# Strassen's algorithm for the output matmul of a fused attention and SwiGLU kernel on one Trainium2 core

## The chip, the core and the metric

The kernel runs on one core of a Trainium2 chip. The metric is device time in microseconds (us), as the median of several runs. "Span" is the time from the first to the last instruction in the trace of one profiled run; it is some 1.8 us shorter than the time that the same run reports. PE is TensorE's matmul stream, PEld its weight loads, DVE is VectorE, ACT is ScalarE, POOL is GpSimd, SP is SyncE. PSUM is the memory to which TensorE writes its results (the tiles `ps_D` of the traces), in banks; SBUF is the memory from which it reads. An eviction is VectorE's copy of a result out of PSUM.

## The reference

Sigmoid attention over 8 batches of 12 heads (448 tokens, 64 columns each), then a SwiGLU feed-forward layer on the 3584 tokens of 768 columns:

```python
scores = scale * np.matmul(q, k.transpose(0, 1, 3, 2)) - np.log(S)
attn_out = np.matmul(1.0 / (1.0 + np.exp(-scores)), v)
x = attn_out.transpose(0, 2, 1, 3).reshape(B * S, H * D)      # 3584 x 768
g = x @ w_gate                                                # 768 -> 1536
out = (g * sigmoid(g) * (x @ w_val)) @ w_out                  # 1536 -> 768
```

## The kernel before

The program is one long stream of matmuls on TensorE with everything else fitted beside it. For each pair of batches `pb` it computes two blocks of the first feed-forward matmul (12 units `ffn1(b, f)` per batch) and then the output matmul (7 units `ffn2(pb, m)`, one per tile of 128 tokens). The attention is cut into 24 "jobs" of 4 heads with 7 chunks each, and from the second batch on a "visit", usually three or four chunks of attention (two visits make a job), is set between two units whenever a program clock says so. I call the stretches F0 to F7 (first matmul of batch 0 to 7) and O0 to O3 (output matmul of pair 0 to 3).

```python
def ffn2(pb, m):                       # one output tile: 2 halves x 12 = 24 matmuls of 384 columns
    D = Banked("o")                    # a PSUM tile of two banks, out of a ring of four
    for half in range(2):
        for f in range(NF):            # NF = 12
            D.write(nc.tensor.matmul(out=D.t[:, half, :hw],
                                     lhsT=h[:, m * 128:(m + 1) * 128],          # hT of (pb, f)
                                     rhs=wo16[f // FW][:, f % FW, half * hw:(half + 1) * hw], ...), half, ...)
    for half in range(2):              # VectorE scales the bank into SBUF
        D.read(nc.vector.tensor_scalar(out=osb[:, hs], in0=D.t[:, half, :hw], scalar1=HREC, ...), half)
    for i in range(2):                 # stores: GpSimd's queue, SP's at the end
        (nc.sync if last else nc.gpsimd).dma_start(out=dsts[i], in_=osb[i * 64:(i + 1) * 64, :])

def fetch(n):                          # q, k, v of job n from HBM; all from GpSimd's queue
    load(n, 0, G); load(n, 1, G); load_v(n)

def ready(n):                          # casts of q and k on GpSimd, then DMA transposes on SP
    cast(n, 0, G); cast(n, 1, G)
    if n >= NPE:
        trans_dma(n, 0); trans_dma(n, 1)

FU1, FU2 = 2.26, 3.9                   # us booked for a unit
FIRST, PER = f1_end[0] - 5.0, 38.5     # first visit, and the time booked per batch of visits
...
begin[(6, 0)] += [lambda: ready(7)]    # what is issued at which chunk of which job
begin[(6, 4)] += [lambda: fetch(8)]
...
for dur, fn, args in units:            # the weave
    if vi < len(visits) and tcur >= vtime[vi]:
        attn_step(group, pvs)          # visit: attention matmuls, casts of the results to xT on VectorE
        ...
    fn(*args)
    tcur += dur
```

In the traces below each of VectorE, GpSimd and the queues of DMA issues works in program order, so what stands ahead and waits holds up all that stands behind.

## Time and profile before

| | before |
|---|---|
| time, median of 3 | 429.04 us (428.95 to 429.08) |
| span of the profiled run | 426.6 us |
| PE busy | 415.9 us, 97%, 3261 matmuls |
| VectorE busy | 204.9 us, 48% |
| GpSimd busy | 117.5 us, 28% |

The table is part 1 of the profile page. With TensorE busy 97% of the span, this kernel can gain mainly by having fewer matmuls, or by filling the start and the end. The prediction below shows the busy slices, the chain of waits and the timelines that say so.

One measure is used throughout. In an undisturbed stretch of this trace a matmul of 384 columns starts 162.5 ns after the one before it, one of 448 columns 189.2 ns, one of the attention's quarter-array matmuls 47 ns on average. I call **loss** all time between the starts of consecutive matmuls beyond that spacing, summed over a stretch; it is worked out from the matmuls' start times in the trace. Before, the losses are 14.9 us in the start (up to F0), 8.5 us in all the rest.

### The profile page before, as it was taken

The numbers are of one execution on the slowest core, as the hardware profiler recorded it, in microseconds if no ns is written. First come the engines' busy times: TensorE is split into PE (matmuls) and PEld (weight loads), VectorE is DVE, ScalarE is ACT, GpSimd is POOL, SyncE is SP. The second block draws the span as 40 slices with busy tenths as digits, with TensorE's granted clock in tenths as the row PEclk, the third lists the DMA queues.
The fourth block names the chain that finished last, engine by engine and source line by source line (L and its number), as shares of the span: only waits on it lengthen the run. The fifth ranks groups of instructions, "written<-read, shape, count | busy, mean of one in ns | idle before, by whom it ended". The sixth has DMA issues, their size and how long they took to land.

```text
span 426.6 us, 7903 instructions
## 1 busy us (share of the span) xinstructions
PE 415.9 (97%) x3261; PEld 217.6 (51%) x3261; DVE 204.9 (48%) x337; ACT 211.9 (50%) x291; POOL 117.5 (28%) x167
## 2 busy tenths in 40 slices
PE   6899999999999999999999999999999999999995
PEld 2544544545555444545555544544555545555663
DVE  2726656555324555555323556555433356555322
ACT  4966885654624755656433755746433642222000
POOL 5564346401637346000345545000221100000000
PEclk8799999999999999999999999999999999999999
DMA  8999999995699997500298996600162300000234
GB/s 301 231 277 211 210 190 208 177 247 99 152 218 174 194 174 178 115 0 2 71 229 169 226 193 164 120 0 2 23 131 71 81 0 2 0 2 0 55 94 111
DMA packets 57796, 54.38 MB, mean 127 GB/s; under 512 B 35680, under 2 KB 52448, under 8 KB 57760
## 3 DMA queue, kind: packets, MB, share of 16 engines
q0 software_dynamic: 20896, 39.20, 40.9%
q1 hardware_dynamic: 36512, 14.13, 20.3%
q8 instruction: 25, 0.41, 0.4%
q10 hardware_dynamic: 352, 0.56, 0.4%
q14 instruction: 11, 0.09, 0.1%
HBM read 47.19 MB, written 11.01 MB: 136 GB/s over the span
## 4 chain that ended last, share of the span: by engine, by line
PE 91%; ACT 3%; DVE 2%; issue 1%; DMA 1%; ACTq 0%; DVEq 0%
PE ps_D L256 50%; PE ps_D L296 26%; PE ps_D L197 8%; PE ps_D L228 7%; ACT pt L215 2%; DMA st<-in_q_dram 1%; PE ps_D L171 1%; DVE t L273 1%; ACT s L271 1%; ACT pt L212 1%; DVE T L180 0%; DVE hT L277 0%; DVE xT L237 0%; DVE xT L245 0%; ACT xT L243 0%
## 5 line engine op out<-in xcount | busy, mean ns | idle before, releaser
L215 ACT ACTIVATE pt<-ps_D,sb_t 128x896 f16<-128x896 f32 x148 | 140.3, 1014 | 84.4 <-PE ps_D L197 84.2
L256 PE MATMUL ps_D<-xT,wg 128*128 128x448 f16 x576 | 126.9, 353 | 0.9 <-ACT pt L215 0.5
L256 PE MATMUL ps_D<-xT,wv 128*128 128x448 f16 x576 | 126.4, 352 | 0.0
L296 PE MATMUL ps_D<-wo,hT 128*128 128x384 f16 x672 | 111.8, 326 | 0.0
L273 DVE TENSOR_TENSOR t<-ps_D,s 128x448 f16<-128x448 f32 x96 | 59.9, 624 | 92.3 <-ACT s L271 92.0
L271 ACT ACTIVATE s<-ps_D 128x448 f16<-128x448 f32 x96 | 52.7, 549 | 90.6 <-PE ps_D L256 80.1
L296 PEld LDWEIGHTS <-hT 128*128 128x128 f16 x672 | 64.8, 98 | 46.4 <-issue 4.3
L256 PEld LDWEIGHTS <-wg 128*128 128x128 f16 x576 | 53.7, 98 | 58.5 <-issue 12.4
L256 PEld LDWEIGHTS <-wv 128*128 128x128 f16 x576 | 56.4, 98 | 52.8 <-issue 0.3
L327 DVE TENSOR_SCALAR osb<-ps_D 128x384 f32<-128x384 f32 x55 | 30.7, 558 | 74.2 <-PE ps_D L296 71.0
L277 DVE SCALAR_TENSOR_TENSOR hT<-ps_D,t 128x448 f16<-128x448 f32 x96 | 60.0, 625 | 10.4 <-DVE t L273 0.5
L337 POOL DMA_DIRECT2D out_dram<-osb x42 | 22.4, 537 | 146.1 <-DVE osb L327 146.1
L149 POOL CAST c<-st 128x896 bf16<-128x896 f32 (+1 forms) x42 | 38.8, 936 | 63.1 <-issue 29.6
L197 PE MATMUL ps_D<-T,T 64*64 64x448 bf16 x672 | 47.4, 367 | 2.3 <-ACT T L180 1.1
L228 PE MATMUL ps_D<-pt,v 64*64 64x448 f16 x672 | 36.2, 351 | 0.3 <-ACT pt L215 0.3
L197 PEld LDWEIGHTS <-T 64*64 64x64 bf16 x672 | 16.3, 107 | 25.9 <-issue 18.2
L237 DVE CAST xT<-ps_D 128x448 f16<-128x448 f32 x24 | 15.0, 625 | 29.8 <-PE ps_D L228 23.0
L245 DVE CAST xT<-ps_D 64x448 f16<-64x448 f32 x46 | 28.6, 622 | 0.7
L228 PEld LDWEIGHTS <-v 64*64 64x64 f16 x672 | 19.9, 108 | 13.0 <-issue 1.5
L212 ACT ACTIVATE pt<-ps_D,sb_t 128x448 f16<-128x448 f32 x40 | 23.0, 631 | 0.0
L140 POOL DMA_DIRECT2D v<-in_v_dram x24 | 17.7, 738 | 0.1
L135 POOL DMA_DIRECT2D st<-in_k_dram x20 | 14.7, 736 | 3.1 <-DMA wv<-in_moe_w_val_dram 3.1
(25 smaller groups left out, 59.6 us busy)
## 6 DMA issues: line engine op xcount, KB each, us to landing
st<-in_q_dram POOLq DMA_DIRECT2D x20, 448.0 KB, 4.8
st<-in_k_dram POOLq DMA_DIRECT2D x20, 448.0 KB, 7.0
out_dram<-osb POOLq DMA_DIRECT2D x42, 192.0 KB, 3.1
v<-in_v_dram POOLq DMA_DIRECT2D x24, 224.0 KB, 8.3
wg<-in_moe_w_gate_dram POOLq DMA_DIRECT2D x4, 576.0 KB, 14.4
wv<-in_moe_w_val_dram POOLq DMA_DIRECT2D x4, 576.0 KB, 14.6
wo<-in_moe_w_out_dram POOLq DMA_DIRECT2D x4, 576.0 KB, 14.7
out_dram<-osb SPq DMA_DIRECT2D x12, 192.0 KB, 2.7
```

Source lines behind the costliest of these rows:

```text
L149: (eng.copy if eng is nc.scalar else eng.tensor_copy)(out=t.rearrange("p c h d -> p h c d"), in_=st.rearrange("p h (c d) -> p h c d", c=C) ...
L197: nc.tensor.matmul(out=sc[w * 64:(w + 1) * 64, h2, :S], lhsT=kt[r, w * 64:(w + 1) * 64], rhs=qt[r, :, w * 64:(w + 1) * 64], start=True, st ...
L212: nc.scalar.activation(out=pt[:, h2, :], in_=sc[:, h2, :S], func=SIGM, bias=sb_t, scale=qkscale), h2
L215: nc.scalar.activation(out=pt, in_=sc[:, :, :S], func=SIGM, bias=sb_t, scale=qkscale)
L228: nc.tensor.matmul(out=P[g:g + 64, h2, :S], lhsT=vt[r, h2, c * D:(c + 1) * D], rhs=pt[r, h2, :], start=(c == 0), stop=(c == C - 1),)
L245: nc.vector.tensor_copy(out=o, in_=i)
L256: nc.tensor.matmul(out=D.t[:, i, :S], lhsT=w16[f // FW][:, pr, cs], rhs=xT[(b, pr)], start=(pr == 0), stop=(pr == NP - 1),),
L271: D.read(nc.scalar.activation(out=s16, in_=D.t[:, 0, :S], func=SIGM), 0)
L273: D.read(nc.vector.tensor_tensor(out=t1, in0=D.t[:, 0, :S], in1=s16, op=MULT), 0)
L277: nc.vector.scalar_tensor_tensor(out=hT[(b // 2, f)][:, b % 2, :], in0=D.t[:, 1, :S], scalar=HSC, in1=t1, op0=MULT, op1=MULT),
L296: nc.tensor.matmul(out=D.t[:, half, :hw], lhsT=h[:, m * 128:(m + 1) * 128], rhs=wo16[f // FW][:, f % FW, half * hw:(half + 1) * hw], start ...
L327: nc.vector.tensor_scalar(out=osb[:, hs], in0=D.t[:, half, :hw], scalar1=HREC, scalar2=None, op0=MULT),
```

## The change

Its intent: a pair of token tiles, g and g+3, is computed in one group. With A the activations of the two tiles, split in two halves of the 1536 inner columns, and B the output weights, split two by two, the Winograd form of Strassen's algorithm needs 7 products where the plain one needs 8. A product is 6 matmuls, so a pair takes 42 instead of 48. There are 11 such groups: 2 in O0 (its first pair of tiles stays plain, to let the weights arrive) and 3 each in O1 to O3; the seventh tile stays plain.

The sums of activations are computed while `ffn1` of the odd batch runs: 72 sums on VectorE in units f = 6 to 11, 24 on GpSimd in units 0 to 5. The 8 sums of weights are computed once on VectorE, in O0. All output stores move to SP's queue; loads, output weights and casts get a new order; the transposes of a job stand further behind its casts; some SBUF pools shrink to make room.

```diff
+    def w_sums(s):                                 # 4 sums of 128 x 1152, called for s = 0 and 1
 ...
+        for kind in (3, 2, 1, 4):                  # b22-b12, wT3+b11, b12-b11, b21-wT2
 ...
+            nc.vector.tensor_tensor(out=t, in0=a, in1=b, op=op)
+    def h_sums(pb, f):
 ...
+        if f < HF:
+            work = ((3, a11, a21, SUB),)
+        else:
+            work = ((1, a21, a22, ADD), (2, None, a11, SUB), (4, a12, None, SUB))
+        for kind, a, b, op in work:
 ...
+            (nc.gpsimd if kind == 3 else nc.vector).tensor_tensor(out=t, in0=a, in1=b, op=op)
 ...
+    def ffn2_group(pb, g):
 ...                                                # mm(k, bank, ..): product k; the comments are added
+        mm(1, 0, True, False)                      # product 1 into bank 0: 6 matmuls
+        snap(0, o1, 0)                             # VectorE: scale bank 0 into o1, left half
+        mm(2, 1, True, True)
+        put(1, o1, 0)                              # VectorE: add bank 1 to o1, left half
+        mm(6, 0, False, False)                     # on top of product 1
+        snap(0, o1, 1)
+        mm(5, 1, True, False)
+        snap(1, o2, 1)
+        mm(7, 0, False, False)
+        put(0, o2, 1)
+        mm(3, 1, False, True)
+        put(1, o1, 1)
+        mm(4, 0, False, True)
 ...                                                # stores from SP
+                o_units += [(FU2, ffn2, (pb, g)), (0.0, w_sums, (0,)), (FU2, ffn2, (pb, g + 3)), (0.0, w_sums, (1,))]
 ...
-    FIRST, PER = f1_end[0] - 5.0, 38.5
+    FIRST, PER = f1_end[0] - 5.0, 37.3
 ...
-    begin[(6, 0)] += [lambda: ready(7)]
-    begin[(6, 4)] += [lambda: fetch(8)]
-    begin[(7, 0)] += [lambda: ready(8), lambda: fetch(9)]
+        (5, 4): ((fetch, 7), (w_out, 0)),
+        (6, 0): ((ready, 7), (w_out, 1)),
+        (6, 4): ((fetch, 8), (w_out, 2)),
+        (7, 0): ((ready, 8), (w_out, 3)),
```

## The prediction

> **What bounds the kernel now.** I read the page first: busy share per slice, then the chain of work that ended last, then the groups. After that came the tensor engine's waits and the timeline of three stretches.
>
> ```profile
> PE   6899999999999999999999999999999999999995
> DVE  2726656555324555555323556555433356555322
> PE 91%; ACT 3%; DVE 2%; issue 1%; DMA 1%; ACTq 0%; DVEq 0%
> PE ps_D L256 50%; PE ps_D L296 26%; PE ps_D L197 8%; PE ps_D L228 7%; ACT pt L215 2%; DMA st<-in_q_dram 1%; PE ps_D L171 1%; DVE t L273 1%; ACT s L271 1%; ACT pt L212 1%; DVE T L180 0%; DVE hT L277 0%; DVE xT L237 0%; DVE xT L245 0%; ACT xT L243 0%
> L296 PE MATMUL ps_D<-wo,hT 128*128 128x384 f16 x672 | 111.8, 326 | 0.0
> L327 DVE TENSOR_SCALAR osb<-ps_D 128x384 f32<-128x384 f32 x55 | 30.7, 558 | 74.2 <-PE ps_D L296 71.0
> ```
>
> Except in the first three slices and the last, PE is full. It is 91% of the chain, and the output matmul (L296) is 26%. The tensor engine's own waits sum to about 6 us, nearly all in the first 25 us. So PE instruction count sets the time, and VectorE at 48% has room on average. One matmul's "326 ns" isn't its cost, because matmuls overlap. The cost is the spacing, which the timeline of the last output phase gives through its evictions, one per 12 matmuls:
>
> ```profile
> 395.71 26.49 PE L296 MATMUL ps_D<-wo,hT 128*128 128x384 f16 x162
> 396.88 0.56 DVE L327 TENSOR_SCALAR osb<-ps_D 128x384 f32<-128x384 f32 x1 [1.16 <-PE ps_D L296]
> 398.83 0.56 DVE L327 TENSOR_SCALAR osb<-ps_D 128x384 f32<-128x384 f32 x1 [1.39 <-PE ps_D L296]
> ...
> 422.23 0.48 ACT L316 ACTIVATE oe<-ps_D 64x384 f32<-64x384 f32 x1 [27.89 <-PE ps_D L296]
> 422.75 0.56 DVE L320 TENSOR_SCALAR oe<-ps_D 64x384 f32<-64x384 f32 x1 [1.91 <-ACT oe L316]
> 423.33 0.47 SPq L324 DMA_DIRECT2D out_dram<-oe  x1
> ```
>
> 398.83 - 396.88 = 1.95 us for 12, so **162.5 ns a matmul**. After PE ends at 422.20 a tail of 4.4 us remains to 426.6. An attention visit inside an output phase looks so:
>
> ```profile
> 127.52 0.57 PE L197 MATMUL ps_D<-T,T 64*64 64x448 bf16 x8
> 127.92 1.49 PE L228 MATMUL ps_D<-pt,v 64*64 64x448 f16 x28
> 129.24 0.55 PE L197 MATMUL ps_D<-T,T 64*64 64x448 bf16 x8
> 129.53 0.62 DVE L237 CAST xT<-ps_D 128x448 f16<-128x448 f32 x1 [1.35 <-ACT pt L212]
> 129.72 4.07 PE L296 MATMUL ps_D<-wo,hT 128*128 128x384 f16 x24
> 130.17 1.26 DVE L245 CAST xT<-ps_D 64x448 f16<-64x448 f32 x2
> ```
>
> PE spends 2.2 us (127.52 to 129.72), while VectorE's three casts run from +2.0 to +3.9 us. This order matters below.
>
> **What the Trainium skill says.** (1) "TensorE: Matmul & The Clock Gate", section "Wait — 56ns, not 53.3ns?": spacing is N / 2.4 GHz plus 2.5 ns. For 384 columns that is 162.5 ns; the trace agrees. (2) "VectorE: DVE Perf Modes", section "The perf-mode tier table (the rule you actually need)": tensor_tensor on 16-bit SBUF data runs 2x, with a PSUM operand 1x. In the trace a 448-column op from PSUM takes 625 ns and a 384-column one 558, so 1.04 ns a column plus about 160 ns. A 16-bit copy of 896 takes 623 ns, i.e. half the slope. No SBUF-only tensor_tensor is in this trace. (3) "SBUF — State Buffer", section "Who interferes with whom": a VectorE instruction with two SBUF inputs and a GpSimd instruction that reads SBUF block each other. No VectorE op before has two SBUF inputs, so the trace can't show it; all the new sums do. (4) "TensorE: Matmul & The Clock Gate", section "What's actually happening": after an idle window of about 3.4 us the PE clock halves. The trace agrees loosely: the granted clock is 0.74 in 10 to 20 us, behind the gaps of the start.
>
> **The change part by part.**
> Removed: a pair of token tiles took 48 matmuls, and takes 7 products x 6 = 42. Groups: three in each of pairs 1 to 3, two in pair 0, so 11. 11 x 6 = 66 matmuls x 162.5 ns = **10.7 us off PE**, all of it on the path. This is the ceiling.
>
> Evictions: 7 instead of 4 per group, 33 more x 558 ns = 18 us of VectorE. A product is 6 x 162.5 = 975 ns, and two PSUM banks alternate. Counting from the start of a product's last matmul: eviction starts at +0.36 (first evictions above), ends at +0.92, PE sees it about 0.05 later (as at its first starts behind VectorE: 5.72 to 5.77). The bank is wanted at 7 x 162.5 = +1.14. Slack 0.17 us: undisturbed groups don't stall. Anything that keeps VectorE busy when a group begins does stall it.
>
> Sums of activations: 72 on VectorE (128x384, 16-bit), each 192 / 0.96 + 156 = 356 ns, 26 us in all. They fall in 6 units of each odd block: 1.25 + 3 x 0.36 = 2.32 us of VectorE against 12 x 189 ns = 2.27 us of PE. Just saturated; attention visits there give PE extra time about equal to their casts. With four PSUM tiles I allow 0.6 us, contention with GpSimd casts (0.94 us each) included. GpSimd's 24 sums are off the path.
>
> Sums of weights: 8 of 1152 columns, 576 / 0.96 + 156 = 756 ns. The first four lie behind a plain tile and hide. **The second four don't.** Working through the schedule (unit times against visit times: after the tile pair 0,3 the clock stands at 65.9, the visit was due at 62.9), the visit of job 9 with job 8's casts comes just ahead of them, and the first group just behind. From the visit's start: casts end +3.9, sums +6.9, the first snapshot of bank 0 +7.5. PE has done two products by +2.2 + 1.95 = +4.2 and wants bank 0. **PE waits 3.4 us.** That idles nearly a clock window, so I add 0.3 us as expected value.
>
> The same queueing with casts alone, twice (the first group of pair 1 and the third of pair 2): +4.5 against +4.2, together 0.8 us. Three groups start one three-chunk visit after the former one; their PSUM tile comes back 0.2 us late: 0.6 at most, I take 0.4.
>
> Schedule: larger units bunch visits. At the turns from pair 1 to 2 and 2 to 3, only one unit lies between visits. In 45 to 60 us, where that is so now, PE lost about 0.2 us per visit; I take 0.6. Transposes now stand behind output stores in SP's queue. Job 17's pair is issued about 2 us after its visit, lands some 6 us later (median 6.1), and is wanted 7.7 us after it: 0.6 us. Loads and output weights move, but I see slack of several us, so 0.
>
> Tail: two output tiles are stored at the end instead of one half tile. SP issues five stores at about 0.5 us each from the end of the last product, the last one near +2.0 instead of +1.1, with about 790 KB in flight: +1.1 us.
>
> Sum: -10.7 + 3.4 + 0.3 + 0.8 + 0.4 + 0.6 + 0.6 + 0.6 + 1.1 = -2.9 us, or 426.1. The losses are estimates that can overlap (PE waiting for one thing lets the others catch up), while the 10.7 us is sure. So I discount them by about a fifth and put the point at **424.6 us**.
>
> **The rivals.**
> A: the sums hide. The author tuned the visit spacing (38.5 to 37.3) for this, VectorE is half idle, and undisturbed groups have slack. Then only the tail and some tenths are lost: 418.5 to 420. Against it speaks the queue order ahead of the first group.
> B: VectorE becomes the bound in odd blocks, through sums slower than 356 ns (1x, or blocked by GpSimd), and groups stall at every bank change. At 1x a sum would take 556 ns, a unit 2.9 us, and 18 such units would give back 18 x 0.65 = 11 us: 429 to 432. The 623 ns copy speaks for 2x.
> C: SP's single queue delays stores or transposes; a missed transpose is several us of idle PE at one or two visits: 427 to 429. Now transposes land in 6 us with 12 between visits, so only the bunched turn is at risk.
>
> **Range and chances.** My sum is a mixture between A and C: 424.6, with 420.3 to 428.0 eight times in ten. Faster by over 2% needs 420.46, so losses under 2.2 us in all; with the weight sums' stall alone at 3.4 that needs my queue reading to fail: 0.14. Slower by over 2% needs B in full: 0.02. Within 2%: 0.84.
>
> **What would show it.** L296's successors should count 606 matmuls with the same spacing. PE busy falls by nearly 11 us, its idle rises by the losses. One idle of about 3.4 us, near 115 to 120 us, released by VectorE right behind the weight sums, confirms the main step; if it is absent I was wrong there, towards A. Sums of 356 and 756 ns confirm 2x; longer ones point to B. Waits inside groups without a visit ahead would refute the slack of 0.17. A PE wait for a transposed tile shows C. The tail behind the last matmul should be about 5.5 us.

## The result, and the profile after

The time is **429.68 us** (median of 4 runs, 429.44 to 429.92), beside 429.06 us for the kernel before in the same rounds (4 runs, 428.95 to 429.84). Ratios are from the fast runs of both kernels in the same rounds, and not quite the ratios of the medians: here 1.0011, with a 95% interval of 0.9993 to 1.0028. Executions over 1.5% slower than the fastest of the same kernel are left out of the means. The change gained nothing. "Within 2%" was right; the point of 424.6 us and the range to 428.0 us were wrong.

Part 1 of the page, first of the kernel before, then of the kernel after (busy us, share of the span, instructions):

```profile
PE 415.9 (97%) x3261; PEld 217.6 (51%) x3261; DVE 204.9 (48%) x337; ACT 211.9 (50%) x291; POOL 117.5 (28%) x167
```

```profile
PE 408.9 (95%) x3195; PEld 212.0 (50%) x3195; DVE 256.3 (60%) x450; ACT 212.0 (50%) x291; POOL 117.7 (27%) x149
```

The 66 matmuls are gone, and PE's busy time fell by 7.0 us, less than the 10.7 us of 66 x 162.5 ns. The span of the profiled run still grew, from 426.6 to 428.1 us. So PE now waits. Parts 2 and 4 of the page of the kernel after say where (busy tenths in 40 slices of 10.7 us each, and the chain that ended last):

```profile
PE   6899999998979999999999999999999999999994
DVE  2726656578664555558765456558865456558753
PE 76%; DVE 12%; ACT 6%; issue 3%; DMA 1%; DVEq 0%; ACTq 0%
```

PE has new dents in the tenth slice (96 to 107 us, the end of F1) and the twelfth (118 to 128 us, in O0), and apart from the last slice (the tail) nowhere else that this view resolves. The chain that set the end went through VectorE for 2% of the span before, and does for 12% now. PE's waits by releaser in the kernel after (sum in us, times, longest); the lines of the start are left out:

```profile
PE ps_D L376 <- DVE osb L387: 3.0, 3, 2.6
PE ps_D L207 <- DMA T<-c: 1.6, 1, 1.6
...
PE ps_D L449 <- DVE xT L255: 0.5, 1, 0.5
...
PE ps_D L207 <- DVE osb L462: 0.4, 1, 0.4
```

L376 is a matmul of a group, L207 one of the attention's q k matmuls, L449 one of a plain output tile. The first two lines are the largest new waits, one behind VectorE and one behind a transposed tile.

The losses by stretch, before and after:

| stretch | before, us | after, us | difference |
|---|---|---|---|
| start and F0 | 14.90 | 15.25 | +0.35 |
| F1 | 0.92 | 3.25 | +2.33 |
| O0 | 0.92 | 5.94 | +5.02 |
| F2, F3 | 2.31 | 3.63 | +1.32 |
| O1 | 0.91 | 1.07 | +0.16 |
| F4, F5 | 1.84 | 3.38 | +1.54 |
| O2 | 1.14 | 1.13 | -0.01 |
| F6, F7, O3 | 0.47 | 1.01 | +0.54 |
| sum | 23.40 | 34.66 | +11.26 |

The last matmul starts at 421.87 before and 422.40 after: -10.73 us of matmuls and +11.26 us of losses make the +0.53 us. The tail behind the last matmul grew from 4.4 to 5.4 us. That is the whole +1.5 us of the two spans. Four places make up most of the losses.

**The stall behind the weight sums (2.7 us, and 1.6 us after it).** The timeline of the kernel after around its first group (start, duration, engine, line, operation; in brackets the idle time before and its releaser):

```profile
117.58 0.61 DVE L247 CAST xT<-ps_D 128x448 f16<-128x448 f32 x1
...
118.22 1.25 DVE L255 CAST xT<-ps_D 64x448 f16<-64x448 f32 x2
...
119.50 0.76 DVE L319 TENSOR_TENSOR wT<-wo,wo 128x1152 f16<-128x1152 f16 x1
...
120.30 0.76 DVE L319 TENSOR_TENSOR wT<-wT,wo 128x1152 f16<-128x1152 f16 x1
120.97 0.75 DVE L319 TENSOR_TENSOR wT<-wo 128x1152 f16<-128x1152 f16 x1
121.64 0.75 DVE L319 TENSOR_TENSOR wT<-wo,wT 128x1152 f16<-128x1152 f16 x1
122.31 0.55 DVE L387 TENSOR_SCALAR osb<-ps_D 128x384 f32<-128x384 f32 x1
122.91 4.71 PE L376 MATMUL ps_D<-wT,S 128*128 128x384 f16 x18 [2.58 <-DVE osb L387]
```

VectorE casts the visit's result, then computes four weight sums, and only then takes the first product out of its bank. PE, which had two products done, waits 2.58 us. From 124.2 us on, ten matmuls start 320 ns apart instead of 162.5, another 1.6 us. The windows view of 122 to 126 us shows a mean granted clock of 0.77 there (the number before the last two). First the kernel after in the profiled run of the result, then the same kernel in the profiled run of e5 (columns: window, length, busy us of PE, PEld, DVE, ACT, POOL with counts, clock, DMA share, GB/s):

```profile
122.00:126.00 4.00, 3.09 (x14) 1.69 (x14) 2.24 (x5) 0.00 (x0) 0.17 (x1) 0.77 1.19 223
```

```profile
122.00:126.00 4.00, 4.00 (x27) 2.40 (x25) 2.18 (x5) 0.00 (x0) 2.24 (x3) 1.00 0.38 83
```

In e5 the stall cost the same 2.74 us between matmul starts, and the clock stayed at 1.00. So whether the clock is lost differs from run to run in this kernel. The traces show what goes with it. The recorded clock changes only at points that lie a multiple of 3.41 us apart, and where these points lie differs from run to run. In the kernel after the clock was halved for exactly one such period:

```profile
124.20:127.60 3.40, 3.40 (x13) 1.67 (x11) 1.00 (x2) 0.00 (x0) 1.77 (x2) 0.50 0.52 101
```

In the period before it, 120.78 to 124.19, PE was idle for 2.13 us. In e5 a point at 120.63 cut the same wait in two, and no period held more than 1.65 us of it. The long waits of the experiments fit: 2.19 us of idle time in one period in e2 and 2.54 in e3 were followed by a half clock, 1.86 at most in e4 (a wait of 2.97 us, cut in two) was not. In the start, where the matmuls are smaller, periods with 1.65 us of idle time were enough. This is read from traces, five waits in all; no run moved a wait on purpose.

**The late tile (1.7 us).** The GpSimd timeline of the kernel before, at the loads of job 8, and then of the kernel after:

```profile
60.49 0.72 POOL L135 DMA_DIRECT2D st<-in_q_dram  x1
```

```profile
60.41 0.79 POOL L124 DMA_DIRECT2D wo<-in_moe_w_out_dram  x1
71.18 0.91 POOL L339 TENSOR_TENSOR S<-hT 128x384 f16<-128x384 f16 x1 [9.98 <-DVE hT L289]
...
75.75 0.75 POOL L144 DMA_DIRECT2D st<-in_q_dram  x1
...
97.62 0.57 PE L207 MATMUL ps_D<-T,T 64*64 64x448 bf16 x8 [1.57 <-DMA T<-c]
```

Before, GpSimd issues the load at 60.49. After, three sums stand ahead of it in GpSimd's queue, and they need `hT` of block 1, which isn't there yet: GpSimd is idle for 9.98 us and issues the load at 75.75. Two more sums, also waiting for `hT`, stand ahead of the casts of job 8, which run at 81.17. So the transpose of k is issued at 83.54 (before: 69.52). It landed 14.0 us later at 97.58, and PE waited for it. Before, nothing in GpSimd's queue waited for TensorE's work there, and it ran ahead. Whether a transpose issued so late is still in time depends on how long it takes to land, and that varies between traces: 14.0 us here, 14.7 in e2, 12.9 in e5 and 12.4 in e4, for waits of 1.6, 2.2, 0.3 and none.

**Sums blocked by casts (0.7 us here).** The timeline of the kernel after at the end of F1:

```profile
98.24 0.93 POOL L159 CAST c<-st 128x896 bf16<-128x896 f32 x1 [9.71 <-DMA st<-in_q_dram]
98.35 1.03 DVE L339 TENSOR_TENSOR S<-hT,hT 128x384 f16<-128x384 f16 x1
...
99.41 0.94 POOL L159 CAST c<-st 128x896 bf16<-128x896 f32 x1 [0.24 <-DMA st<-in_k_dram]
99.41 1.14 DVE L339 TENSOR_TENSOR S<-S,hT 128x384 f16<-128x384 f16 x1
...
100.58 0.36 DVE L339 TENSOR_TENSOR S<-hT,S 128x384 f16<-128x384 f16 x1
```

A sum takes 0.36 us alone. One of these that starts inside a GpSimd cast ends about 0.2 us after that cast, so it takes up to 1.14 us. The casts of the visit stand behind these sums, and the next output tile waits for them (the 0.5 us of L449 above). The first four weight sums met two GpSimd casts in the same way: two of them took 1.48 us instead of 0.76, and the visit behind them waited 0.4 us (L207 behind L462 above).

**The full odd blocks (2.3 us in F3 and F5).** There the same sums fill VectorE to the brim. No single wait is above 0.7 us; the losses of the blocks grew by 1.3 and 0.9 us. F7 has the same 18 sums but no attention visits any more, and shows VectorE's pace (`t` opens the gate of each unit):

```profile
388.93 0.62 DVE L285 TENSOR_TENSOR t<-ps_D,s 128x448 f16<-128x448 f32 x1
...
391.37 0.62 DVE L285 TENSOR_TENSOR t<-ps_D,s 128x448 f16<-128x448 f32 x1
```

A unit with three sums takes VectorE 2.44 us against PE's 2.27. VectorE falls some 1.0 us behind in F7's six units, and yet F7 lost nothing (0.00 us): presumably the four PSUM tiles took it up. So in this trace the sums cost PE time only where a visit with its casts falls among them. In F3 it was hardly the blocking by GpSimd: of its 18 sums one was longer than 0.36 us, by 0.20. In F5 two were, by 0.89 together, so there the two causes stay mixed.

### The profile page after: what moved, and what is told of

It is laid out like the page before. It is cut to its first block, busy times and chain, and to the rows that moved or that the text cites. A ratio compares the mean times of both kernels' runs of the same rounds, so it can differ in the third digit from the quotient of the medians.

```text
span 428.1 us, 7939 instructions
## 1 busy us (share of the span) xinstructions
PE 408.9 (95%) x3195; PEld 212.0 (50%) x3195; DVE 256.3 (60%) x450; ACT 212.0 (50%) x291; POOL 117.7 (27%) x149
## 4 chain that ended last, share of the span: by engine, by line
PE 76%; DVE 12%; ACT 6%; issue 3%; DMA 1%; DVEq 0%; ACTq 0%
PE ps_D L266 41%; PE ps_D L376 17%; PE ps_D L207 6%; PE ps_D L238 6%; PE ps_D L449 5%; ACT pt L225 4%; DVE S L339 3%; DVE t L285 3%; DVE hT L289 2%; DVE xT L255 1%; ACT s L283 1%; DVE wT L319 1%; PE ps_D L181 1%; DMA st<-in_q_dram 1%; DVE xT L247 1%
## 5 line engine op out<-in xcount | busy, mean ns | idle before, releaser
L159 POOL CAST c<-st 128x896 bf16<-128x896 f32 (+1 forms) x42 | 39.8, 957 | 111.6 <-DMA T<-c 47.3
L289 DVE SCALAR_TENSOR_TENSOR hT<-ps_D,t 128x448 f16<-128x448 f32 x96 | 60.0, 625 | 10.5
L339 POOL TENSOR_TENSOR S<-hT 128x384 f16<-128x384 f16 x24 | 21.8, 912 | 147.4 <-DVE hT L289 147.3
L207 PE MATMUL ps_D<-T,T 64*64 64x448 bf16 x672 | 47.6, 367 | 4.9 <-DMA T<-c 1.6
L376 PE MATMUL ps_D<-wT,S 128*128 128x384 f16 x198 | 35.6, 336 | 3.0 <-DVE osb L387 3.0
L376 PEld LDWEIGHTS <-S 128*128 128x128 f16 x264 | 26.4, 100 | 21.7 <-issue 5.2
L387 DVE TENSOR_SCALAR osb<-ps_D 128x384 f32<-128x384 f32 x43 | 24.0, 558 | 20.0 <-PE ps_D L376 19.5
L207 PEld LDWEIGHTS <-T 64*64 64x64 bf16 x672 | 16.3, 107 | 29.4 <-issue 20.1
L393 DVE SCALAR_TENSOR_TENSOR osb<-ps_D,osb 128x384 f32<-128x384 f32 x33 | 18.4, 558 | 13.8 <-PE ps_D L376 13.5
L376 PEld LDWEIGHTS <-hT 128*128 128x128 f16 x198 | 18.9, 98 | 14.2 <-issue 2.1
L449 PE MATMUL ps_D<-wo,hT 128*128 128x384 f16 x144 | 24.2, 326 | 0.9 <-DVE xT L255 0.5
```

The costliest lines, as they stand in the source:

```text
L159: (eng.copy if eng is nc.scalar else eng.tensor_copy)(out=t.rearrange("p c h d -> p h c d"), in_=st.rearrange("p h (c d) -> p h c d", c=C) ...
L207: nc.tensor.matmul(out=sc[w * 64:(w + 1) * 64, h2, :S], lhsT=kt[r, w * 64:(w + 1) * 64], rhs=qt[r, :, w * 64:(w + 1) * 64], start=True, st ...
L289: nc.vector.scalar_tensor_tensor(out=hT[(b // 2, f)][:, b % 2, :], in0=D.t[:, 1, :S], scalar=HSC, in1=t1, op0=MULT, op1=MULT),
L339: (nc.gpsimd if kind == 3 else nc.vector).tensor_tensor(out=t, in0=a, in1=b, op=op)
L376: nc.tensor.matmul(out=D.t[:, bank, :hw], lhsT=l, rhs=B_(i), start=(first and i == 0), stop=(i == HF - 1), skip_group_check=True,),
L449: nc.tensor.matmul(out=D.t[:, half, :hw], lhsT=h[:, m * 128:(m + 1) * 128], rhs=wo16[f // FW][:, f % FW, half * hw:(half + 1) * hw], start ...
```

## The experiments

Ten runs, all with five timed rounds beside the kernel before on the same chip. e1 to e4 ran on one chip, e5 to e10, in two sets, on another. The theory on trial: the 10.7 us are real, and PE gives them back at the four places named, through queue order on VectorE and GpSimd. The rivals: the reordering of loads and stores costs by itself, or the groups do, or the next wait takes the place of each that is removed.

### e1: the reordering without Strassen

```diff
-        if b % 2:
-            h_sums(b // 2, f)
 ...                                                # last tile stored half by half, as before
-                o_units += [(FU2, ffn2, (pb, g)), (0.0, w_sums, (0,)), (FU2, ffn2, (pb, g + 3)), (0.0, w_sums, (1,))]
+                o_units += [(FU2, ffn2, (pb, g)), (FU2, ffn2, (pb, g + 3))]
             else:
-                o_units.append((FU3, ffn2_group, (pb, g)))
+                o_units += [(FU2, ffn2, (pb, g)), (FU2, ffn2, (pb, g + 3))]
-    FIRST, PER = f1_end[0] - 5.0, 37.3
+    FIRST, PER = f1_end[0] - 5.0, 38.5
```

> The change without Strassen: plain products in all pairs, no sums, but its buffers, load order, stores from SP and transposes behind half a job kept. Theory (the losses come from the sums and from the queues they stand in): about as before, ratio to before 0.998 to 1.003, no tensor engine wait for a transposed tile near 95 us. Rival (the reordering itself costs, the smaller pools or the shared SP queue): 1.005 or more, with waits for transposes or loads in the trace.

Measured: 428.42 us (428.11 to 429.13), ratio 0.9990 [0.9975, 1.0004]. The losses are 23.63 us, as before (23.40), and the wait for the tile is gone. The run takes out the sums and the groups together and puts the visit spacing back as well (e10 tests that). So stores on SP, the smaller pools, the new order of loads and the split transposes cost nothing by themselves. The late tile needs GpSimd's sums.

### e2: weight sums ahead of the plain tiles

```diff
-                o_units += [(FU2, ffn2, (pb, g)), (0.0, w_sums, (0,)), (FU2, ffn2, (pb, g + 3)), (0.0, w_sums, (1,))]
+                o_units += [(0.0, w_sums, (0,)), (FU2, ffn2, (pb, g)), (0.0, w_sums, (1,)), (FU2, ffn2, (pb, g + 3))]
```

> The eight weight sums moved one plain tile earlier each, so that none stands between the casts of job 8 and the first group. Theory: the wait of 2.6 us at 120 us falls to about 0.4, the ten matmuls at half clock behind it go (1.6 us), so 4 to 4.8 us less than the changed kernel: about 425, granted clock near 1.00 in 122 to 130 us. Rival (losses are interchangeable, the next wait takes its place): under 2 us gained.

Measured: 427.21 us (424.98 to 430.99), ratio 0.9969 [0.9934, 1.0003]. In O0 the loss fell from 5.94 to 1.34 us: stall and slow matmuls are gone, which shows that the queue order on VectorE made them. But F1 lost 4.87 us instead of 3.25. PE's largest wait in e2's trace is now the tile's, and the clock of the window of 96 to 100 us is 0.81:

```profile
PE ps_D L207 <- DMA T<-c: 2.2, 1, 2.2
```

```profile
96.00:100.00 4.00, 1.89 (x27) 1.03 (x31) 3.68 (x8) 1.46 (x3) 1.39 (x2) 0.81 0.75 210
```

The 28 attention matmuls at 98.51 took 2.82 us instead of 1.49. So the halved clock appeared at another stall, and took back part of the gain. The runs spread over 6 us.

### e3: the loads of job 8 ahead of GpSimd's sums

```diff
-        (6, 0): ((ready, 7), (w_out, 1)),
-        (6, 4): ((fetch, 8), (w_out, 2)),
+        (6, 0): ((ready, 7), (fetch, 8)),
+        (6, 4): ((w_out, 1), (w_out, 2)),
```

> Job 8's loads are put into GpSimd's queue ahead of the sums of the odd block, the output weights behind them. Theory: the load then starts near 61 us instead of 76, the transposed tile of job 8 is there in time, the 1.6 us wait at 96 us goes: 1.3 to 1.9 us less than the changed kernel, about 428. Rival (the DMA queues are full there anyway, and the transposes still land late): under 0.5 us.

Measured: 428.99 us (427.34 to 429.90), ratio 0.9997 [0.9980, 1.0014]. The wait for the tile is gone, as expected, but not in the way that I had thought, and nothing was gained: F1 lost 3.24 us as in the kernel after. The loads of job 8 were issued at 60.20, but its casts still stand behind GpSimd's sums, and the transpose of k was issued at 83.15, hardly sooner than the 83.54 of the kernel after. It landed in 11.7 us instead of 14.0. As it took 12.4 to 14.7 us in four traces with the old order of loads, this may be chance. The timeline of e3 at the same place:

```profile
96.00 1.03 DVE L339 TENSOR_TENSOR S<-S,hT 128x384 f16<-128x384 f16 x1
...
99.50 0.57 PE L207 MATMUL ps_D<-T,T 64*64 64x448 bf16 x8 [1.93 <-DVE hT L289]
```

The loads of the next job, issued at 86.00 (after: 86.32), landed sooner too, in 9.8 us instead of 11.9, so GpSimd's casts of them began at 95.89 instead of 98.24, in the midst of VectorE's sums. Two sums took 1.03 and 1.12 us, the gate of that unit (L289) came late, and PE waited 1.93 us for it. My expectation of a gain of 1.3 to 1.9 us missed; the rival, that the next wait takes the place, held. The tile and the blocked sums are two waits at one place, and removing one alone showed nothing.

### e4: no activation sums on VectorE (a wrong result)

```diff
-            work = ((1, a21, a22, ADD), (2, None, a11, SUB), (4, a12, None, SUB))
+            work = ()
 ...
-            return lambda i: (hS[(pb, kind, i)][:, cs], None)
+            return lambda i: (hS[(pb, 3, i)][:, cs], None)
```

> Wrong result on purpose: the 72 activation sums on VectorE are left out, their products use GpSimd's sum instead. GpSimd's sums, weight sums, evictions and all matmuls stay. Theory: VectorE's saturation in the second half of the odd blocks costs some 2.5 us (0.5 near 101 us, 1.0 near 198 to 208, 0.7 near 297 to 308 and small ones), so 427.0 to 427.6. Rival 1 (the 0.17 us of slack in the groups is the cost, through the 33 more evictions): no gain at all. Rival 2 (saturation is worse than the waits show): 4 us or more.

Measured: 426.00 us (423.15 to 429.36), ratio 0.9937 [0.9898, 0.9977]; the relative error of the output is 2.05, as intended. In the profiled run, which was the fastest (423.15), F1 fell to 0.92 us, F3 to 1.40 and F5 to 1.14. Part of F1's fall is chance: the late tile landed just in time in this trace. The rest, 0.6 in F1, 1.3 in F3 and 0.7 in F5, is 2.6 us that VectorE's sums cost PE directly. O0 fell too, from 5.94 to 4.04 us: the stall behind the weight sums was still there (2.97 us), but no half clock followed it, and the visit ahead wasn't held up. That part says nothing of the activation sums. The median gained more than I expected (427.0 to 427.6). The spread of 6 us stayed, with the two slowest runs at a lower clock (0.985 and 0.986 against 0.992).

### e5: the kernel after once more

> The changed kernel once more, for the spread on this chip: e2 spread from 425.0 to 431.0 us and e4 from 423.2 to 429.4, the slower of them at a lower granted clock. If the lateness of job 8's tile and the half clock behind a wait of over 2 us are a matter of chance, this one spreads too, by 2 us or more; if it is steady as in its first four runs (0.5 us), the spread comes with the experiments.

There is no edit. Measured: 429.15 us over the five fast runs (426.81 to 431.53), ratio 0.9997 [0.9961, 1.0033]; a sixth run took 433.75 us. It counts as slow because it is 1.6% above the fastest; its clock was 0.983. As this kernel's own stalls lower the clock too, it may not be another state of the chip. So the result repeats, and the kernel after spreads over several us where the four runs of the result had seemed tight. The kernel before spread by 3.1 us in the same rounds (428.31 to 431.45), though by 1.5 us on the chip of e1 to e4, so part of the spread may be the chip's. The profiled run took 426.81 us. Its losses are 2.15 us in F1 and 4.28 in O0, against 3.25 and 5.94 in the first trace: 2.8 us of the 3.1 us between the two spans (425.0 and 428.1). The halved clock was absent, and the tile came only 0.3 us late. Neither is in the trace of the kernel before. The clock doesn't explain every slow run: the slowest of e2 (430.99 us) had 0.989, where its profiled run (426.61 us) had 0.990. Only profiled runs have a trace, so what each of the others lost isn't known.

### e6: weight sums early, and jobs 7, 8 and 9 loaded and cast ahead of GpSimd's sums

```diff
 ...                                                # with the edit of e2
-        (6, 0): ((ready, 7), (w_out, 1)),
-        (6, 4): ((fetch, 8), (w_out, 2)),
-        (7, 0): ((ready, 8), (w_out, 3)),
-        (7, 4): ((fetch, 9),),
-        (8, 0): ((ready, 9), (fetch, 10)),
+        (6, 0): ((ready, 7), (fetch, 8), (w_out, 1), (ready, 8), (fetch, 9)),
+        (6, 4): ((w_out, 2),),
+        (7, 0): ((ready, 9), (w_out, 3)),
+        (7, 4): ((fetch, 10),),
```

> e2 (weight sums early), and in GpSimd's queue the loads and casts of job 8 and the loads of job 9 stand ahead of the sums of the odd block, the casts of job 9 ahead of VectorE's sums. Theory: both the wait for job 8's tile and the blocking of VectorE's sums by GpSimd's casts (1.0 to 1.1 us instead of 0.36 each, at 96 to 99 us) go, the loss in block 1 falls from 3.3 to about 1.2 us, and the spread to under 1 us, for no wait over 1 us is left to halve the clock: 422 to 423.5. Rival (losses are interchangeable): 425 or more, another wait in 90 to 110 us.

Measured: 424.31 us (423.81 to 424.69), ratio 0.9879 [0.9858, 0.9900]. F1 lost 1.89 us, O0 1.25 us. The time is a little above the 422 to 423.5 us that I expected, as F1 kept more than the 1.2 us of the theory: a cast of job 9 and a sum of GpSimd's now met two of VectorE's sums near 90 us, which took 0.63 and 1.66 us, and VectorE was still behind when PE waited 0.57 us for a gate at 98.5 us. The spread is down to 0.9 us. With both stalls gone, no wait in the middle of the program is long, and the runs agree. That fits the reading that the spread came from the clock and the late tile; it doesn't show it, as the slow runs left no trace, and the kernel before, without such waits, spread by 3.1 us in these rounds.

### e7: VectorE's sums spread out

```diff
-            (nc.gpsimd if kind == 3 else nc.vector).tensor_tensor(out=t, in0=a, in1=b, op=op)
+            if kind == 3:
+                nc.gpsimd.tensor_tensor(out=t, in0=a, in1=b, op=op)
+            else:
+                todo.append((t, a, b, op))
+        do_sums(2)                                  # at most two per unit; the rest ahead of the plain tile
 ...
     def ffn2(pb, m):
+        do_sums(len(todo))
```

This is e6 with the sums deferred: 18 sums per odd block, two per unit at most from unit 6 on, the last six ahead of the plain output tile, which comes first in each output stretch.

> e6, and VectorE does at most two activation sums in each unit of the odd block, the last six in the plain tile behind it. Theory (saturation of VectorE in those units): about 1.0 to 2.0 us less than e6, most of it in blocks 3 and 5, about 421. Rival (the waits there come from the casts of the visits, not from the sums): under 0.5 us.

Measured: 421.06 us (five runs, 420.70 to 421.79), ratio 0.9807 [0.9781, 0.9833], 3.2 us below e6, where I had expected 1 to 2. F1, F3 and F5 lose 0.92, 1.41 and 1.14 us, as in e4 where there are no such sums. Sums were still blocked: F3's 18 took 8.9 us in all instead of 6.7 in the kernel after, and cost nothing. So VectorE at 60% on average was enough for all the sums; three of them per unit were too many where a visit fell among these units.

### e8: half of the last stores from GpSimd

```diff
-            eng.dma_start(out=dsts[i], in_=o1[i * 64:(i + 1) * 64, :])
+            (nc.gpsimd if end and i else eng).dma_start(out=dsts[i], in_=o1[i * 64:(i + 1) * 64, :])
 ...
-                eng.dma_start(out=dsts[i][:, hw:], in_=o2[i * 64:(i + 1) * 64, hw:])
+                (nc.gpsimd if i else eng).dma_start(out=dsts[i][:, hw:], in_=o2[i * 64:(i + 1) * 64, hw:])
```

> e7, with two of the five last stores of SP issued from GpSimd instead. Theory (SP's issue time of 0.5 us a store makes the longer tail): the tail behind the last matmul falls from 5.4 to about 4.6 us, so 0.4 to 0.9 us less than e7. Rival (the tail is the transfer itself): no difference.

Measured: 423.49 us (422.85 to 426.01), ratio 0.9873, so 2.4 us worse than e7. The theory, that SP's one queue of stores makes the longer tail, is refuted as an advice: with two queues the last store was indeed issued 1.57 us after the last matmul's start instead of 2.50, but it landed no sooner (5.0 against 4.7 us after it), as each store took longer. From the DMA view of e8 at the end (KB each, median us from issue to landing):

```profile
out_dram<-osb POOLq DMA_DIRECT2D x1, 192.0 KB, 3.9
out_dram<-osb SPq DMA_DIRECT2D x1, 96.0 KB, 4.0
```

In e7 these stores took 2.5 to 2.9 us. And the program ended 2.2 us after the last landing, not 1.0 us as in e7. The tail grew from 5.4 to 6.9 us. Most of the rest of the difference lies in O0, which lost 2.2 us instead of 1.45 (see e9).

### e9: halves stored as soon as they are summed

```diff
         put(1, o1, 0)
+        if end:
+            store(rows1, o1, 0)                     # SP stores the left half of tile g
 ...
         put(0, o2, 1)
+        if end:
+            store(rows2, o2, 1)                     # right half of tile g+3
 ...
         put(1, o1, 1)
 ...
+        if end:
+            store(rows1, o1, 1)                     # right half of tile g
```

> e7, and in the last group each half of a tile is stored from SP as soon as it is summed: two halves go out during the group, one beside the last product, one behind it, as before the change. Theory (too many stores are queued on SP at the end): the tail behind the last matmul falls from 5.45 to about 4.5 us, ratio about 0.979 against 0.981 for e7. Rival (the early stores hold the tile that VectorE still adds to, and stall the group): the tail falls, but waits of over 1 us appear inside the last group.

Measured: **420.62 us** (420.00 to 421.26), ratio 0.9796 [0.9773, 0.9819]. This is the lowest median of all, 2.0% below the kernel before; the interval reaches across 2%, and overlaps that of e7, so the step from e7 isn't clear of noise. The tail is 4.25 us, shorter than before the change, and no wait appeared inside the last group (O3 lost 0.00 us), so the rival is out. The page of e9, busy tenths and chain:

```profile
PE   6899999999999999999999999999999999999995
PE 84%; DVE 6%; ACT 6%; issue 2%; DMA 1%; DVEq 0%; ACTq 0%
```

The dents are gone, and VectorE's share of the chain has halved. In its profiled run O0 lost 2.22 us (e7: 1.45), through a wait of 0.92 us that ended at 105.92 us, which e8's trace also has (0.88 us) and e7's hasn't. The timelines show what made it: in e9 a deferred sum started at 102.18 us, just behind a GpSimd cast of 102.15, and took 1.11 us, so that VectorE came to the plain tile at 105.32 instead of 104.72. In e7 the data of that cast had landed sooner, it ran at 100.76, and met no sum there.

### e10: visits spread again

```diff
-    FIRST, PER = f1_end[0] - 5.0, 37.3
+    FIRST, PER = f1_end[0] - 5.0, 38.5
```

> e9 with the attention visits spaced as before the change (38.5 instead of 37.3), so that no two visits have only one unit between them at the turn from pair 2 to 3. Theory (bunched visits cost): the losses in blocks 4 and 6 fall from 1.52 and 1.01 us towards the 0.92 and 0.47 of before, up to 1 us in all, ratio about 0.977. Rival (the tuned spacing is there for a reason): the transposed tiles or the casts come late elsewhere, no gain or a loss.

Measured: 421.33 us (420.29 to 424.73), ratio to the kernel before 0.9825 [0.9791, 0.9859], against 0.9796 for e9. The bunching in F4 went (1.52 to 0.92 us), as the theory says. In F6 it didn't (1.01 to 1.20 us): two visits with one unit between them stayed at the turn from pair 2 to 3, so the edit did only half of what I expected. O1 and O2 lost 0.5 and 1.2 us more; more visits fall among their groups now. The rival held: the two spacings come to the same within the noise.

The losses side by side, in us, each from the profiled run:

| | after | e2 | e3 | e4 | e6 | e7 | e9 |
|---|---|---|---|---|---|---|---|
| F1 | 3.25 | 4.87 | 3.24 | 0.92 | 1.89 | 0.92 | 0.92 |
| O0 | 5.94 | 1.34 | 5.50 | 4.04 | 1.25 | 1.45 | 2.22 |
| F2, F3 | 3.63 | 3.41 | 3.73 | 2.32 | 3.94 | 2.33 | 2.32 |
| F4, F5 | 3.38 | 3.40 | 3.29 | 2.66 | 3.32 | 2.66 | 2.66 |
| all | 34.66 | 31.33 | 33.90 | 27.88 | 28.92 | 25.78 | 26.38 |
| tail | 5.4 | 5.4 | 5.4 | 5.4 | 5.4 | 5.4 | 4.25 |

## Why the prediction was right or wrong

It was right about the removed matmuls, about most of the places that lose and about the class, and wrong in the point by 5.1 us: it forecast a gain of 4.4 us, and there was none. The step that failed is its sum of losses. Its losses with the tail came to 7.8 us ahead of the discount, and the profiled run has 12.3 us (11.26 and 1.0).

What held:
- **The ceiling of 10.7 us.** 66 matmuls are gone, and the spacing in undisturbed groups is still 162.5 ns.
- **The slack of 0.17 us.** Groups without a visit or sums ahead have no wait. The rival in which groups stall at every bank change is out: O3 lost 0.00 us.
- **The durations.** An unblocked activation sum takes 0.36 us and an unblocked weight sum 0.76 (predicted 356 and 756 ns). Between 384 and 1152 columns that is 0.52 ns a column, half of the 1.04 of operations on PSUM, so the sums run at the 2x rate. The prediction's 16-bit copy of 623 ns reads PSUM, and so spoke only weakly for it.
- **The weight sums' stall.** It is where the prediction put it, behind the casts and four sums, released by the first eviction; e2 shows the cause. The size was 2.6 us instead of 3.4. VectorE had the first product out of its bank 7.5 us after the visit's start (122.86 against 115.39), just as predicted; but the visit itself was held up by 0.6 us, so PE wanted the bank that much later. Where it wasn't held up (e3, e4) the wait was 2.97 us.
- **The tail**, +1.0 us for +1.1 predicted; e9 gives it back.
- **Bunched visits**: +0.60 in F4, which e10 takes back, and +0.54 in F6, which it doesn't. That is 1.1 us for 0.6 predicted, but F6 also holds more attention than before (84 of its matmuls instead of 40), so not all of it need be bunching.

What failed:
- **"Loads and output weights move, but I see slack of several us, so 0".** I looked at where the loads stand in the program, not at what stands ahead of them in GpSimd's queue. The sums there wait for a block that comes 10 us later, so the loads of job 8 were issued 15 us later than before and its transposes 14 us later, which used up the slack. It cost 1.7 us in the first trace, by a landing time that varies. e1 shows that the reordering without these sums is free, and e6 that the wait can be removed.
- **"With four PSUM tiles I allow 0.6 us, contention with GpSimd casts (0.94 us each) included".** It was about 3.5 us: 0.7 at the end of F1, 1.3 in F3, 0.9 in F5, and 0.6 through the blocked weight sums. The prediction had named both causes, a saturated unit (2.32 against 2.27 us) and the interference of the engines, and then gave each too little. e4 and e7, which take the sums out and spread them, bring F1, F3 and F5 back to their losses before or within 0.25 us of them. The step that failed in F3 and F5 is "attention visits there give PE extra time about equal to their casts": a unit took VectorE 2.44 us and not 2.32, F7 with the same sums and no visits lost nothing, and the blocks with visits lost 1.3 and 0.9 us. In F3 blocking lengthened the sums by 0.2 us only; in F5, with 0.9 us, the share of blocking stays open.
- **"I add 0.3 us as expected value" for the clock.** In the first trace it cost 1.6 us, in e5 nothing. As a chance it can't be called wrong from a few traces: after this stall the clock fell in two of four (the kernel after and e3, not e4 and e5). But two stalls were there to set it off, not one. And the prediction took the start of the trace for a loose confirmation of the page's idle window, though the longest wait there was 1.2 us.
- **The discount by a fifth.** The reason given was that losses overlap. Here they didn't: they lay at different places of the stream, and what PE had lost at one, nothing returned at the next. The undiscounted sum, 426.1 us, would have been nearer, though still too low. (A slip without effect: in rival B, 18 x 0.65 is 11.7 us, not 11.)
- **Predicted and not there:** the late PSUM tile in visits of three chunks (0.4 us predicted, 0.05 at most found) and the transposes of job 17 behind the stores (0.6 predicted, none). The two waits of groups behind casts came as predicted, 0.39 and 0.41 us, but O1 and O2 as a whole lost only 0.15 us more than before, as they hold less attention than before.

The working goes up, then: 1.7 for the tile, 1.3 for the clock, 2.9 for the sums, 0.5 for the bunching and 0.4 for the start; and down by 0.7 for the stall, 1.0 for the two that weren't there, 0.7 for the groups behind casts and 0.1 for the tail. This is +4.3 us of the 4.5 us between 7.8 and 12.3.

The rivals of the prediction fared so. A (the sums hide) was wrong for this order of the program and is nearly right for e9, which reaches 420.6 us. C (a transposed tile is late) was right, but by GpSimd's queue and not SP's. B was right as to the engines that block one another, and wrong as to the 2x rate and the size.

## What to carry to other kernels

An average share of 48% on the engine that takes the new work says nothing about the units in which it falls: book the work unit by unit against what TensorE does in that unit, with the visits that fall there, and defer what doesn't fit to the next stretch with room. When an engine that also issues loads or casts gets work that waits for data, follow each load behind it in that engine's queue to its first reader. And a stall that goes at one place can come back at the next in the stream (e2, e3), so remove stalls that lie close together in one step before judging any of them.

## What the Trainium skill lacked or had wrong

- "TensorE: Matmul & The Clock Gate", section "What's actually happening", gives the half clock after at least one idle window of about 3.4 us. The length agrees: the recorded clock changed at points 3.41 us apart, and was halved for 3.41 us at a time in the middle of the program. But the window didn't have to be idle throughout. Outside the start, periods with 2.13, 2.19 and 2.54 us of idle PE were followed by a half clock (the kernel after, e2, e3), those with 1.86 us and less were not (e4, e5). So single waits of 2.2 us were at risk here, which the page doesn't say.
- "SBUF — State Buffer", section "Who interferes with whom", says that a VectorE instruction with two SBUF inputs and a GpSimd instruction that reads SBUF block each other. The trace agrees, but the page gives no cost for this pair. Here an activation sum of 0.36 us took 1.03 to 1.14 us beside a cast of 0.93 us, as it ended only about 0.2 us after the cast; a weight sum of 0.76 us took 1.48.
- I found no page that tells what two stores from GpSimd's queue among the last ones do to the end of a program. In e8 the last stores took 3.4 to 4.0 us from issue to landing, those from SP and ScalarE too, against 2.2 to 2.7 in e7, and the program ended 2.2 us after the last landing instead of 1.0.
